# A sequence-mixing kernel's convolution: the last inverse stage by blocks of 32 channels, four product buffers, decays by products, and new order constants

## The chip, the cores and the metric

The kernel runs on one core of a Trainium2 chip. The metric is the device time of one execution in microseconds. The kernel before takes 688.63 us, the median of 3 runs (688.52 to 689.50). The engines are named as in the profile: PE (matrix products), DVE (vectors), ACT (scalar functions), POOL (general purpose) and SP, which issues most transfers.

## The reference

A block of a network on one sequence of 2048 positions and 512 channels: a long convolution per channel, whose taps come from 128 decaying oscillations a channel, and after it a mixer of four dense layers. Cut to what matters:

```python
x = A_u                                                # [1, 2048, 512]
n = layernorm(x)
dt = exp(log_dt); A = -exp(log_A_real) + 1j * A_imag   # [512, 128]
C = (C_real + 1j * C_imag) * dt[:, None]
K = 2 * einsum("dn,dnl->dl", C, exp((A * dt)[:, :, None] * arange(2048))).real
y = irfft(rfft(n, 4096) * rfft(K, 4096))[:2048]        # along the sequence
h = x + y + n * D_skip
out = h + B_ref(layernorm(h))      # two layers with shifts, then 512 -> 1792 -> 512
```

## The kernel before

The kernel has two phases. `conv_phase` computes `h`, which stays on the core as 16 tiles of 128 x 512; `mixer_phase` does the rest. The mixer starts with the last four tiles of `h` (`finish(3)`, `norm1(3)`, `turn1(3)`), so these are on its way first.

**Taps.** The 512 channels are done in 32 chunks of 16 (`table(g)`, `taps(s, g)`). The 2048 positions are split in two factors, so a chunk needs two small tables of sines and cosines times decays: ACT makes `pt` (sines and cosines of integer phases that POOL adds up), DVE or POOL multiply them by `amx` and `amy` into `cs` and `sn`, and PE multiplies the two tables into `kt`, 16 channels' taps. `SHARE` says which chunks' operations go to POOL or ACT instead of DVE: `amy`, `csy` and `sny` name chunks whose product is POOL's, `sq` chunks in which ACT squares part of `amx`. A list holds indices in a group of eight; the first list is for step 0 (`g < 8`), the second for all others. The decays are exponentials of the rates: `rates()` makes six for the low digits (`eb`) and, later, three for the high digits (`ec[:, :, 1]` to `ec[:, :, 3]`, with factors 512, 1024 and 1536). ACT's exponentials and its sines are in different table sets, which it has to load.

**Steps.** The channels are convolved in four steps of 128 (`WID`). In each the transform is done in two stages. `spectra_of_taps(s)` does stage A of the taps, by blocks of 64 channels, into `at[:, 1]`: either `stage_a_turn` (DVE transposes) or two `stage_a_taps` (more, smaller matmuls and copies by ACT); `SHARE["turn"]` lists the blocks of the first kind, by index 2s + r. `stage_a_x` does stage A of the input into `at[:, 0]`. For steps 2 and 3 (`FAR`) the input's whole spectrum is computed early (`spectrum_x`), sent to memory and fetched by `back`. Then for each of eight groups of frequencies `e`, `product(s, e)` does stage B on PE and multiplies both spectra into a buffer `u` (four partial products of a complex product), and `stage_b_inv(s, e)` transforms back into `at[:, 0]`. There are two buffers `u0` and `u1`, used in turn. `SHARE["sum..."]` lists the `e` whose four partial products are summed to two on DVE or POOL before; PE then needs two terms instead of four. `SHARE["mul..."]` lists the `e` whose product is POOL's.

After the eight groups `stage_a_inv` (steps 0 to 2) turns blocks of 32 channels on DVE into `u0` or `u1` and adds the last stage's result to `h`. The last step has `last_a_inv`: four transposes on DVE (`turn_inv`, r = 0 to 3, 32 channels each), then for each quarter `q` of the positions (in the order 3, 0, 1, 2) one product with the identity (`keep`) that puts `h` into a PSUM bank, four matmuls over 512 columns that add all 128 channels, and a copy to `h`. `q = 3` also goes through the statistics (`part`) that the mixer's first tiles need.

**x.** `norm_x()` takes the mean and variance of the 16 tiles on DVE, computes one root for all, and normalises: `SHARE["nrm"]` names two tiles for POOL, DVE takes the other four with j < `LND`, ACT ten.

**Order.** Nothing is issued as it stands in the source. `Plan.add` collects the instructions with a cost, what they read and write, and for some a constant `at`; `Plan.order` then places them engine by engine, and the engines run them in that order. Among an engine's instructions that can start within `LOOK` (0.05) of the earliest, it takes the one with the smallest due time, which is

```python
a["late"] = min([1e9 if a["at"] is None else a["at"]] + [N[j]["late"] - lag for j in succ[i]])
```

so the constants in `NOM` only rank instructions. `TS[s]`, the base of step s, is `t0` plus s times `per`; taps of step 0 are due at `kg0`, those of others at `TS[s - 1] + kg + ...`, the taps' stage A at `TS[s] - ak`, products at `TS[s] + b e`, inverses `ib` later, the early spectra at `xa + xs n`, the last stage's `keep` at `TS[4] + 15 + n` and its matmuls at `TS[4] + 20 + n`. Where PE would idle the plan puts matmuls with the identity as fillers, so that its clock stays up. PSUM banks are handed out by the plan; two pairs and two single ones are there.

## Time and profile before

| | us |
|---|---|
| median of the runs | 688.63 |
| the profiled execution | 688.2 |
| its span | 686.4 |
| PE busy | 650.4 |
| DVE busy | 547.6 |
| ACT busy | 408.0 |
| POOL busy | 404.9 |
| DVE busy from 0 to 305 | 274.8 |
| mean granted PE clock | 0.993 |

The convolution is roughly the first 305 us. All instructions of both phases carry the line L87, that of the helper through which they are issued, so groups are told apart by the tiles that they write and read: `pt`, `cs`, `sn`, `amx`, `amp` (which holds `amy`), `kt`, `at`, `u`, `bs`, `h`. `bank` is PSUM. A row of the timeline or of the chain starts with its start and duration; in a group's row stand count, busy time and mean in nanoseconds, then the idle time just before and what ended it. A row of the windows has the window and its length, the busy time of PE, PEld (weight loads), DVE, ACT and POOL, the granted clock, the share of the DMA engines and GB/s. A matmul of this type of number shows as two records.

### The profile page before, as it was taken

How to read it: one execution, taken by the hardware profiler on the slowest of the kernel's cores; microseconds unless marked ns; L12 is line 12 of the kernel's file. 1: busy time of each engine (PE TensorE's matmuls, PEld its weight loads, DVE VectorE, ACT ScalarE, POOL GpSimd, SP SyncE). 2: the span in 40 equal slices, each digit the busy share in tenths (PEclk: the TensorE clock that was granted, in tenths of full speed). 3: DMA queues.
4: the chain of work that ended last, by engine and by line, in shares of the span. 5: the costliest groups of instructions: out<-in, count | busy, mean ns of one | idle time of the engine just before them, and what ended most of it. 6: DMA issues, size and time to landing. Idle time of an engine off the chain costs nothing.

```text
span 686.4 us, 16787 instructions
## 1 busy us (share of the span) xinstructions
PE 650.4 (95%) x6806; PEld 507.3 (74%) x6806; DVE 547.6 (80%) x952; ACT 408.0 (59%) x706; POOL 404.9 (59%) x422
## 2 busy tenths in 40 slices
PE   5987989999999997999999999999999999999997
PEld 5885756663677584748888888888888888888885
DVE  5998899999897998989978798866879954455554
ACT  7889878967889876245634555544365443444330
POOL 1889589968999999002576209355635555554210
PEclk9998999999999999999999999999999999999999
DMA  8930554011301133020231311133311342211004
GB/s 224 268 128 2 168 174 110 3 48 32 64 3 49 34 95 110 1 63 1 62 93 48 106 32 47 46 97 103 96 44 46 101 129 62 62 46 47 21 11 122
DMA packets 49266, 51.49 MB, mean 75 GB/s; under 512 B 6437, under 2 KB 33061, under 8 KB 49189
## 3 DMA queue, kind: packets, MB, share of 16 engines
q1 hardware_dynamic: 47524, 47.80, 24.3%
q10 hardware_dynamic: 1152, 1.57, 0.9%
q0 software_dynamic: 512, 1.05, 0.6%
q8 instruction: 53, 0.87, 0.5%
q14 instruction: 25, 0.20, 0.1%
HBM read 35.72 MB, written 8.39 MB: 64 GB/s over the span
## 4 chain that ended last, share of the span: by engine, by line
PE 61%; ACT 13%; DVE 13%; POOL 4%; issue 4%; DMA 3%; SPq 2%; ACTq 0%; DVEq 0%; POOLq 0%
PE l L87 24%; PE acc L87 11%; ACT pt L87 8%; PE bank L87 6%; DVE u L87 4%; PE l3a L87 3%; PE l3g L87 3%; PE l3d L87 3%; PE l3f L87 3%; PE l3e L87 3%; PE l3c L87 3%; PE l3b L87 3%; DVE at L87 2%; SPq L347 2%; DVE cs L87 2%
## 5 line engine op out<-in xcount | busy, mean ns | idle before, releaser
L87 ACT ACTIVATE pt<-pt 128x1056 f32<-128x1056 int32 x64 | 69.8, 1091 | 14.5 <-POOL pt L87 6.3
L87 POOL TENSOR_TENSOR pt<-p,s 128x512 int32<-128x512 int32 x64 | 71.8, 1139 | 5.1 <-DVE sn L87 4.0
L87 PE MATMUL bank<-at,tbs 128*64 128x128 f32 (+1 forms) x768 | 63.1, 311 | 3.3 <-DVE u L87 1.8
L87 PEld LDWEIGHTS bank<-at,tbs 128*64 128x64 f32 x768 | 44.5, 134 | 20.6 <-ACT at L87 3.0
L87 PEld LDWEIGHTS bank<-ident 128*128 128x128 f32 x418 | 51.0, 200 | 8.3 <-issue 5.1
L87 PE MATMUL bank<-ident 128*128 128x128 f32 x418 | 55.1, 289 | 0.0
L87 PE MATMUL bank<-u,ms 64*128 64x128 f32 x768 | 50.6, 280 | 3.5 <-DVE at L87 1.3
L87 PEld LDWEIGHTS bank<-u,ms 64*128 64x128 f32 x768 | 45.4, 187 | 8.2 <-issue 1.8
L87 POOL TENSOR_TENSOR cs0w<-raw,cs0w 128x512 fp32r<-128x512 f32 x7 | 9.1, 1296 | 59.0 <-ACT cs0w L87 59.0
L87 DVE TENSOR_TENSOR cs<-pt,amx 128x512 f32<-128x512 f32 x64 | 40.9, 677 | 2.5 <-ACT pt L87 1.3
L87 DVE TENSOR_TENSOR h<-h,l 128x512 f32<-128x512 f32 x48 | 32.1, 684 | 11.0 <-PE l L87 11.0
L87 PEld LDWEIGHTS bank<-cs 128*32 128x32 f32 x1024 | 24.2, 111 | 22.5 <-POOL cs L87 6.1
L87 PE MATMUL bank<-cs 128*32 128x64 f32 x1024 | 32.7, 225 | 8.4 <-DVE cs L87 4.1
L87 POOL TENSOR_TENSOR sn1w<-raw,sn1w 128x512 fp32r<-128x512 f32 x7 | 9.5, 1359 | 52.1 <-ACT sn1w L87 41.7
L87 DVE TENSOR_TENSOR u<-u,l3f 128x512 f32<-128x512 f32 x14 | 9.5, 682 | 36.9 <-PE l3f L87 36.9
L87 ACT COPY at<-bank 128x512 f32<-128x512 f32 x40 | 24.9, 630 | 23.1 <-PE bank L87 23.0
L87 ACT ACTIVATE pt<-pt,halfpi 128x1056 f32<-128x1056 f32 x32 | 38.1, 1191 | 0.5
L87 POOL TENSOR_TENSOR sn<-pt,amp 128x512 f32<-128x512 f32 x30 | 36.8, 1227 | 1.4 <-ACT pt L87 1.1
L87 DVE STREAM_TRANSPOSE at<-bank 128x512 f32<-128x512 f32 (+1 forms) x40 | 35.6, 922 | 1.9 <-PE bank L87 1.9
L87 ACT ACTIVATE u<-u 128x512 f32<-128x512 f32 x56 | 35.4, 632 | 1.8
L87 PE MATMUL bank<-sn 128*32 128x64 f32 x1024 | 32.0, 223 | 2.5 <-DVE sn L87 2.5
L87 POOL TENSOR_TENSOR cs<-pt,amp 128x512 f32<-128x512 f32 x26 | 31.9, 1227 | 3.6 <-PE bank L87 1.1
(1159 smaller groups left out, 2082.9 us busy)
## 6 DMA issues: line engine op xcount, KB each, us to landing
raw<-in_B_w_dram SPq DMA_DIRECT2D x28, 256.0 KB, 2.8
xq<-xq SPq DMA_DIRECT2D x72, 64.0 KB, 2.0
h<-in_A_u_dram SPq DMA_DIRECT2D x32, 128.0 KB, 3.8
h<-in_A_u_dram SPq DMA_DIRECT2D x16, 256.0 KB, 4.1
rawa<-in_B_w_dram SPq DMA_DIRECT2D x14, 256.0 KB, 2.8
rawb<-in_B_w_dram SPq DMA_DIRECT2D x14, 256.0 KB, 2.9
ms<-in_mm_dram SPq DMA_DIRECT2D x4, 768.0 KB, 10.1
out_dram<-h SPq DMA_DIRECT2D x48, 64.0 KB, 1.7
```

The lines of the kernel that those rows point to most:

```text
L87: ins = f(*args, **kw)
L347: dma = lambda d, s: lambda: nc.sync.dma_start(d, s)
```

## The change

- **Last inverse stage.** `last_a_inv` issues all four `keep`, then the matmuls by blocks: for each r the four quarters q, over 128 columns (4 positions x 32 channels) instead of 512. A block needs only its own transpose; the bank is complete after r = 3.
- **Product buffers.** In the last step the `u` buffers are four: `thp` and `ini`, the phases' parameters, serve as the third and fourth once the tables are done.
- **High decays.** Only the factor 512 is an exponential, issued with the six others ahead of the first sine. The second is its square on ACT, the third the product of both on POOL. The later exponentials, and the change to their table set and back, go.
- **Parameters.** The first block's three copies out of PSUM go from ACT to DVE.
- **Statistics and normalisation of x.** `LNA = 4`: four tiles' sums and sums of squares are ACT's (two passes each). `LND = 4`, and no tile is normalised by POOL.
- **Shares.** `amy`, `csy`, `sny` and `sq` have a list for each step. In the last step the sums of e = 0, 1, 2, 5 go to POOL, those of 4, 6, 7 stay on DVE and 3 has none; the product of e = 4 goes to POOL. Step 0 loses the sums of e = 1 and 3. Block 2 (the first of step 1) is no longer turned by DVE.
- **Order.** `ak`, `ax`, `b`, `ib`, `y`, `ys`, `kg` and `kgs` get an addend for each step (`nom(n, s)`), the bases `TS` one for steps 1 to 3, and all constants have new values.

The diff, without the lines that only replace `NOM[...]` by `nom(...)`:

```diff
-SHARE = {'nrm': [[1], [5]], 'mul0': [[0], [7]], 'mul2': [[6], []], 'amy': [[0, 1, 3, 4, 5, 6, 7], [1, 2, 3, 6]], 'csy': [[1, 4, 5, 6, 7], [0, 1, 2, 3, 4, 5, 7]], 'sny': [[1, 2, 3, 5, 6, 7], [0, 1, 2, 3, 4, 5, 6, 7]], 'sq': [[0, 1, 5, 7], [0, 2, 3, 4, 6, 7]], 'turn': [[1, 2, 3, 5, 6, 7], [2, 3, 5, 6, 7]], 'hadd': [[0, 1, 2, 7], [0, 1, 2, 3, 5, 6, 7]], 'sum0': [[3], [1, 4, 6]], 'sum1': [[], [0]], 'sum2': [[], [4, 5, 6]], 'sum3': [[0, 1, 2, 3, 4, 5, 6, 7], []]}
+SHARE = {'nrm': [[], []], 'mul0': [[2], [7]], 'mul2': [[6], [4]], 'amy': [[0, 1, 2, 3, 4, 5, 6, 7], [0, 1, 2, 3, 6], [0, 2, 4, 6, 7], [3, 4, 6, 7]], 'csy': [[2, 3, 5, 6], [0, 1, 2, 3, 4, 5, 7], [0, 1, 2, 3, 4, 5, 7], [0, 1, 2, 3, 4, 5, 7]], 'sny': [[1, 2, 3, 5, 6, 7], [1, 2, 3, 4, 6, 7], [0, 1, 2, 3, 4, 6], [0, 1, 2, 3, 4, 5, 6, 7]], 'sq': [[0, 1, 2, 6], [0, 2, 3, 4, 5, 6, 7], [0, 1, 2, 4, 5, 6, 7], [0, 1, 3, 4, 5, 6, 7]], 'turn': [[1, 3, 5, 6, 7], [2, 3, 5, 6, 7]], 'hadd': [[0, 1, 2], [0, 1, 2, 3, 5, 6, 7]], 'sum0': [[], [4, 6]], 'sum1': [[], [0]], 'sum2': [[], [3, 4, 6]], 'sum3': [[4, 6, 7], [0, 1, 2, 5]]}
...
-LND = 5
-LNA = 0
+LND = 4
+LNA = 4
...
-NOM = {'t0': 20909.27, 'per': -2434.34, 'ln': 6742.44, 'kg0': -2181.49, 'kgs0': 3.82, 'kg': 15568.18, 'kgs': 8895.14, 'ak': 3925.33, 'ax': 241.48, 'b': 3.78, 'ib': -3456.91, 'y': 7609.31, 'ys': 1528.17, 'tr': 11007.37, 'exp': 6791.26, 'wt': 19369.85, 'pr1': 14609.18, 'pr2': 19765.45, 'st': 18836.53, 'xa': 5533.7, 'xs': -976.95}
+NOM = {'lna': -6411.31, 't0': 20522.35, 'per': -894.26, 'ln': -5822.64, 'kg0': -9318.19, 'kgs0': 3.78, 'kg': -2101.91, 'kgs': 25013.05, 'ak': 17752.48, 'ax': -220.66, 'b': 524.38, 'ib': -1943.3, 'y': 24805.75, 'ys': 7260.8, 'tr': 18844.68, 'exp': -1591.78, 'wt': 30586.62, 'pr1': 48035.89, 'pr2': 11141.85, 'st': 33977.18, 'xa': 4397.29, 'xs': -1767.73, 'kg.1': 38137.64, 'kg.2': 11471.49, 'kg.3': -9808.59, 'kgs.1': 22767.09, 'kgs.2': -6950.05, 'kgs.3': -1943.45, 'ak.0': -192.4, 'ak.1': 10223.63, 'ak.2': -15787.22, 'ak.3': 7962.67, 'ax.0': -11988.2, 'ax.1': 7758.29, 'ax.2': -8412.62, 'ax.3': 24117.63, 'b.0': 182.31, 'b.1': 415.63, 'b.2': -299.98, 'b.3': 33.97, 'ib.0': 152.15, 'ib.1': -1799.03, 'ib.2': 11285.45, 'ib.3': 39936.16, 'y.0': 12856.89, 'y.1': 6177.68, 'y.2': 23800.04, 'y.3': -15848.95, 'ys.0': -8274.72, 'ys.1': 11499.17, 'ys.2': -20246.8, 'ys.3': -37984.55, 't.1': 15629.02, 't.2': 3507.55, 't.3': 7837.49}
...
+    TS = [t + NOM.get(f"t.{i}", 0) for i, t in enumerate(TS)]
+    nom = lambda n, s: NOM[n] + NOM[f"{n}.{s}"]
...
-    decays += [(ec[:, :, k], 512.0 * k) for k in range(1, 4)]
+    decays += [(ec[:, :, 1], 512.0)]
...
-            for i, (d, m) in enumerate(decays[6:]):
-                add("ACT", 0.99 if i else 2.3, lambda d=d, m=m: act.activation(d, plan.view(p), AF.Exp, scale=-m), r=["lam"], w=["trig"], at=NOM["exp"])
-            add("ACT", 1.45, sine, w=["trig", "ex"], at=NOM["exp"], frees=p)
+            add("ACT", 0.99, lambda: act.activation(ec[:, :, 2], ec[:, :, 1], AF.Square), w=["ex"], at=NOM["exp"])
+            add("POOL", 1.2, lambda: gp.tensor_tensor(ec[:, :, 3], ec[:, :, 1], ec[:, :, 2], ALU.mult), w=["ex"], at=NOM["exp"])
...
+    uu += [t.rearrange("p g i d -> p (g i d)") for t in (thp, ini)]
+    PARAM = [("A", t) for t in R4] + [("I", t) for t in R4]
+
+    def turn_of(s, e):
+
+        k = e % (4 if s + 1 == NS else 2)
+        return uu[k], [("u", k)] + (PARAM if k > 1 else [])
...
-            def mm(q=q, view_=view_):
-                for c in R4:
-                    i = c % 2 * 16 + q * 4
-                    pe.matmul(view_()[quarter(c)], fis[:, c // 2, :],
-                              g[:, :, i : i + 4, :].rearrange("p d i t -> p i d t"), start=not KEEP, stop=True)
...
+        def mm(q, r):
+            b = plan.view(ps[q])[:, 0 : 4 * w_].rearrange("p (j d) -> p j d", j=4)
+            for c in R4:
+                i = c % 2 * 16 + q * 4
+                pe.matmul(b[quarter(c), :, r * 32 : r * 32 + 32], fis[:, c // 2, :],
+                          g[:, r * 16 : r * 16 + 16, i : i + 4, :].rearrange("p d i t -> p i d t"), start=False, stop=r == w_ // 32 - 1)
+
+        for r in range(w_ // 32):
+            for n, q in enumerate((3, 0, 1, 2)):
+                i = add("PE", 0.32, lambda q=q, r=r: mm(q, r), r=[("g", r), "fis"], w=[("hq", q)], at=TS[s + 1] + 20 + 4 * r + n)
...
-        a0 = 16 - LNA
-        for j in range(a0):
+        for j in range(LNA, 16):
             add("DVE", 0.6, lambda j=j: v.bn_stats(bx[:, j, :], h[:, j, :]),
...
-            for j in range(a0, 16):
+            for j in range(LNA):
                 add("ACT", 0.62, lambda j=j: act.activation(junk, h[:, j, :], AF.Copy, accum_out=sm[:, j : j + 1]),
-                    r=[("x", j // 2, c) for c in R4], w=[("u", 0), "sm"])
+                    r=[("x", j // 2, c) for c in R4], w=[("u", 0), "sm"], at=NOM["lna"])
```

96 lines of the change are left out of this document (48 added, 48 removed).

## The prediction

> **What bounds the kernel now.** I read the windows first, cut where the stages change, to see which engine is busiest in each; then the groups of instructions for prices, the chain of waits for 45 to 75 us, and the timeline of the last step.
>
> ```profile
> span 686.4 us, 16787 instructions
> ...
> 20.00:45.00 25.00, 22.49 (x307) 21.82 (x306) 23.96 (x61) 20.08 (x37) 20.39 (x23) 1.00 0.74 242
> 45.00:75.00 30.00, 25.11 (x495) 18.75 (x495) 26.77 (x36) 27.69 (x49) 28.39 (x25) 0.89 0.16 37
> 75.00:100.00 25.00, 23.40 (x568) 16.61 (x566) 22.87 (x52) 18.35 (x34) 15.94 (x17) 1.00 0.54 178
> 100.00:250.00 150.00, 140.41 (x2910) 94.47 (x2908) 138.24 (x204) 126.08 (x222) 134.64 (x133) 1.00 0.18 49
> 276.00:295.00 19.00, 18.53 (x257) 15.21 (x250) 18.42 (x31) 4.88 (x8) 0.00 (x0) 1.00 0.01 2
> 305.00:686.00 381.00, 376.95 (x1676) 311.28 (x1674) 272.83 (x473) 176.70 (x298) 176.84 (x191) 1.00 0.23 64
> ```
>
> The columns are PE, PEld, DVE, ACT, POOL. From 305 us to the end PE is 99% busy and the change leaves that code alone, so whatever moves the moment at which the mixer's first transposes start (304.79, below) moves the end by as much. Ahead of it, DVE is busiest (24.0 of 25 us, then 138.2 of 150), with POOL close behind (134.6 of 150). Much of PE's share there is filler, so its digits are no bound. The stretch 45 to 75 is ACT's and POOL's. In the last step DVE has 18.4 of 19 us and POOL nothing. So I count what each edit adds to DVE, POOL and ACT in each stretch.
>
> **Part 1, up to 75 us.** Four of 16 statistics go to ACT, two normalisations from POOL to ACT, high decays lose two exponentials and two table loads.
>
> ```profile
> L87 DVE BATCH_NORM_STATS2 bs<-h 128x6 f32<-128x512 f32 x16 | 10.4, 662 | 0.0
> L87 POOL TENSOR_SCALAR h<-h,mvh,bs 128x512 f32<-128x512 f32 x2 | 4.1, 2070 | 0.0
> L87 ACT COPY at<-bank 128x512 f32<-128x512 f32 x40 | 24.9, 630 | 23.1 <-PE bank L87 23.0
> L87 ACT ACT_TABLE_LOAD x4 | 5.1, 1283 | 0.8 <-PEq L1639 0.7
> L87 ACT ACTIVATE ec<-bank 128x512 f32<-128x512 f32 x3 | 3.2, 1144 | 0.0
> L87 ACT ACTIVATE h<-h,bs 128x512 f32<-128x512 f32 x10 | 7.4, 801 | 0.0
> ...
> 57.33 1.33 POOL h L87
> ...
> 59.41 2.06 POOL h L87
> ...
> 55.00:60.00 5.00, 1.81 (x49) 1.25 (x52) 4.02 (x8) 5.00 (x10) 4.89 (x4) 0.95 0.00 2
> 60.00:65.00 5.00, 4.31 (x64) 2.21 (x56) 3.65 (x8) 4.45 (x12) 5.00 (x5) 0.50 0.01 3
> 65.00:70.00 5.00, 5.00 (x108) 2.21 (x100) 4.58 (x6) 3.59 (x4) 5.00 (x5) 0.87 0.01 3
> ```
>
> DVE loses 4 x 0.66 = 2.65 us ahead of the root that all normalisations wait for, in a stretch where it is 96% busy. POOL loses 2 x 2.07, of which 1.33 + 2.06 = 3.39 us lie on the chain, just ahead of the transforms of x. ACT gains eight passes over 512 elements (price not shown with an accumulated output; between 0.63, the plain copy of that size, and 0.80, the normalisation's: 5.0 to 6.4 us, I take 5.7) and 2 x 0.80; it loses 2 x 1.28 and 2 x 1.14 and gains one squaring, at an exponential's 1.14. Net +3.6 us on an engine with 25 - 20.08 = 4.9 us idle from 20 to 45: that idle time covers it, and without the cover it is rival C. The multiplication on POOL (no longer than a normalisation's 2.07 there) is covered by the 4.1 us that POOL loses. The evacuation of the first parameter block moves three small copies to DVE, idle then; 0. Other shares of step 0 (one amplitude to POOL, one cosine back) cancel within 0.4 us. The two gains are the same wait seen from two sides (earlier root, shorter tail) and ACT's own queue of normalisations is what is late next, so I don't add them: **-2.65**, from -4.4 (-2.65 and the tail less ACT's two, 3.39 - 1.6) to +3.2 (rival C).
>
> **Part 2, steps 1 to 3's tables, 75 to 276 us.**
>
> ```profile
> L87 DVE TENSOR_TENSOR sn<-pt,amp 128x512 f32<-128x512 f32 x2 | 2.2, 1119 | 0.0
> L87 DVE TENSOR_TENSOR amp<-E,ec 128x512 f32<-128x512 f32 x13 | 10.1, 778 | 0.1
> L87 DVE STREAM_TRANSPOSE at<-bank 128x512 f32<-128x512 f32 x24 | 16.1, 703 | 0.0
> L87 DVE TENSOR_TENSOR amx<-E,amx 128x512 f32<-128x512 f32 x22 | 15.2, 691 | 5.9 <-ACT amx L87 5.8
> L87 DVE TENSOR_TENSOR amx<-E,amx 128x896 f32<-128x896 f32 x10 | 10.9, 1091 | 2.7 <-ACT amx L87 2.7
> L87 POOL TENSOR_TENSOR sn<-pt,amp 128x512 f32<-128x512 f32 x30 | 36.8, 1227 | 1.4 <-ACT pt L87 1.1 <-POOL pt L87 0.2
> L87 POOL TENSOR_TENSOR amp<-E,ec 128x512 f32<-128x512 f32 x19 | 21.4, 1131 | 6.0 <-DVE ec L87 5.6
> L87 POOL TENSOR_TENSOR u<-u 128x256 f32<-128x256 f32 x14 | 11.1, 818 | 0.8 <-DVE u L87 0.8
> 131.63 1.62 DVE L87 TENSOR_TENSOR u<-u 128x256 f32<-128x256 f32 x2
> 277.12 0.76 DVE L87 TENSOR_TENSOR u<-u 128x256 f32<-128x256 f32 x2
> ```
>
> DVE: four sine products come back (+4.48), two amplitudes go to POOL (-1.56), one block of taps is turned by PE and ACT instead of four transposes (-2.81), three more chunks leave part of the amplitudes to ACT's squares (3 x (1.09 - 0.69) = -1.20), the sum of e = 3 in step 0 goes (-1.62): -2.7 us. POOL: -4.9 for the sines, about +2.3 for the amplitudes, -1.6 for one pair of sums: -4.2. ACT +2.5 of copies (4 x 0.63) and three pairs of squares (put at DVE's shorter form, 0.69, together +2.1), against 24 us idle from 100 to 250. PE has two more four-term inverses, +2.1, under its fillers. The extra squares hardly add a wait: DVE idles 0.27 us ahead of either form (5.9/22, 2.7/10). DVE is 92% busy from 100 to 250, so -2.7 x 0.92 = -2.5, and 0.2 back for the waits: **-2.3**, from -4.2 (POOL sets the pace) to +1 (ACT's 4.6 us shows by about a quarter in place of the gain).
>
> **The order.** An instruction's due time is the smaller of its own constant and what its followers leave it. Worked out from the constants, the new taps of step 3 are due at 25677.06 - 17752.48 - 7962.67 = -38 and the end at about 16945 + 20; before, 9681 and 11192. Nearly every other new constant lies above what the followers give, so it decides nothing; as before, step 0's tables come first, then what leads to step 3's taps, then the rest. One thing moves: before, the spectra of x for steps 2 and 3 (due 4557 and 5534) went ahead of all tables of step 1; now (2630, 4397) their own constants lie behind and they interleave by length of path. That touches 75 to 100 us, where POOL idles 9 us and ACT 6.7 but DVE only 2.1. DVE's work is the cover: **0**, between -2.1 and +2.1.
>
> **Part 3, the last step, and part 4, its inverse by blocks.**
>
> ```profile
> 276.61 1.10 PE L87 MATMUL bank<-at,tbs 128*64 128x128 f32 x16
> 277.65 1.23 PE L87 MATMUL bank<-u,ms 64*128 64x128 f32 x16
> ...
> 292.96 1.16 PE L87 MATMUL bank<-u,ms 64*128 64x128 f32 x16
> ...
> 294.60 3.60 PE L87 MATMUL bank<-h,ident 128*128 128x512 f32 x8
> 294.80 4.63 DVE L87 STREAM_TRANSPOSE at<-at 128x1024 f32<-128x1024 f32 x4 [0.29 <-ACT at L87]
> ...
> 298.03 0.61 PE L87 MATMUL amx<-ident 128*128 128x128 f32 x4
> ...
> 299.48 4.72 PE L87 MATMUL bank<-at,fis 128*32 128x512 f32 x32 [0.84 <-DVE at L87]
> 300.87 0.89 DVE L87 BATCH_NORM_STATS2 bs<-bank 128x6 f32<-128x128 f32 x4 [1.45 <-PE bank L87]
> 301.19 0.14 PEld L87 LDWEIGHTS bank<-at,fis 128*32 128x32 f32 x4 [0.43 <-issue]
> 304.79 1.99 PE L87 MATMUL xt<-ident,xq 128*128 128x128 f32 x16 [0.59 <-DVE rn L87]
> 53.72 0.29 PE L87 MATMUL bank<-cs 128*32 128x64 f32 x8
> 53.83 0.29 PE L87 MATMUL bank<-sn 128*32 128x64 f32 x8
> ```
>
> DVE is relieved of five pairs of sums and one product, but PE is next: a product's matmuls and an inverse's take 1.04 us each (276.61 to 277.65), and from 276.61 to 294.0 seven of one and eight of the other make 15.6 of 17.4 us. The unsummed e = 3 adds 1.04. So four buffers can win at most 17.4 - 16.6 = 0.8 us; I take **-0.4**. Above: DVE's pair of sums took 1.62 us at 131.63 and 0.76 at 277.12, where POOL had nothing. POOL now works here too; three pairs at 0.86 more give +2.2. The Trainium skill (SBUF — State Buffer, on the shared port pair) says why: a DVE operation with two inputs in SBUF and a GpSimd one that reads SBUF lock each other out for the whole instruction. By that rule alone part 3 would be +2.2; the slower pair agrees, but DVE has the slack now.
>
> Part 4 looks like a gain, since the blocks need not wait for all four transposes. But what each block adds to, the four products with the identity, holds PE from 294.60 to 298.03 and is due earlier than every block. Then PE takes r = 0, 1, 2 for all four q before q = 3's last block, and q = 3 alone feeds the statistics at 300.87. A quarter of the 4.72 us for one r is 1.18: 298.03 + 3.25 x 1.18 = 301.87, where the old q = 3 was done at 299.48 + 1.18 = 300.66. That is **+1.2**. Ends: at the taps' pace (eight records of 64 columns in 0.11 us, 0.88 an r) 300.89, +0.2; with the 0.14 us load bare ahead of every four (0.14 + 0.43/4, twice for each q, 2.0 an r) 304.5, +3.9. A gain (-0.9, the last block 0.3 after the last transpose at 299.43) needs the blocks ahead of the products with the identity.
>
> **Sum:** -2.65 - 2.3 + 0 - 0.4 + 1.2 = -4.15 from the profiled execution's 688.2 (span 686.4 and 1.8 around it): 684.05. The median of the runs is 0.43 above that execution, so **684.5**.
>
> **The rivals.**
> A, *the clock falls at the handover* (0.17). PE would finish its blocks at 298.03 + 4.7 = 302.7 and wait until 304.79 + 1.2 = 306.0. From 55 to 60 us PE was busy 1.8 of 5, and the clock went to 0.50 and 0.87, some 6.8 us at half speed. Ahead of a PE-bound stretch 3.4 to 6.8 us at half cost 1.7 to 3.4: 684.5 + 2.5 = 687.0. Against it: 3.3 us of idle time is near the least that can do it. The Trainium skill (TensorE: Matmul & The Clock Gate, Part 1) puts the window at about 3.4 us, free-running; by that rule the idle time may or may not fill one, and the dip here agrees with it.
> B, *all reliefs count* (0.15): -4.4 - 4.2 - 0.8 + 0.2, 9.2 less, 679.4. For it: DVE and POOL are both lightened. Against: ACT is not.
> C, *the statistics on ACT come last* (0.20), the slower side. They are due behind all of step 0's tables (-6411 against -9318) on an in-order engine. ACT needs 5.7 + 1.6 more; the 4.8 us that the decays free lie ahead of 21 us, when x is still landing. If they can't be used, 7.3 us meet 4.9 idle and ACT is over 90% busy from 45 on, so the normalisation ends 2.4 later, and the small operations that turn sums into moments, put at 0.8, with it: +3.2. DVE's relief is then half waited away (-1.2), and 688.6 + 3.2 - 1.2 - 0.4 + 1.2 = 691.4. It decides from 5 us of ACT work that finds no gap before 45.
> The forecast itself holds 0.48.
>
> **How the numbers follow.** No change can be told within 0.2%, 1.4 us: 687.25 to 690.0. The forecast's own range, 681.5 to 687.5, gives 0.46 faster and 0.02 same; A 0.10 and 0.07; B 0.15; C 0.04 same and 0.16 slower. Together 0.71, 0.13, 0.16. The range runs from just under B to C, 679 to 691.5.
>
> **What would show it.** Part 1: the last normalisation before 60 us and no clock dip there; if the root comes after 40, C. Part 2: DVE some 2.5 us less busy between 75 and 276, with POOL's idle time up. Part 3: products and inverses back to back on PE at 1.04. Part 4: q = 3's statistics about 7.3 us after the first of the four transposes, where 300.87 - 294.80 = 6.1 before; 5.2 would make it wrong. A: a granted clock below 1.00 just after the handover. Two or more of parts 1 to 3 gaining nothing would make the whole wrong.

## The result, and the profile after

The kernel with the change takes 690.11 us, the median of 22 runs (687.15 to 691.99), the kernel before 688.36 in the 22 runs beside them (687.26 to 689.62). The ratio is 1.0022, with an interval of 1.0012 to 1.0033: slower by 1.5 us by the ratio (0.8 to 2.3), 1.75 by the medians. The forecast was 684.5, so the time lies inside the range of 679 to 691.5 and on the wrong side of the time before.

The profiled execution of the changed kernel took 689.71 us. Its windows follow, with the columns of before (PE, PEld, DVE, ACT, POOL, granted clock, DMA share, GB/s). In this kernel the helper's line is L86.

```profile
span 687.9 us, 17248 instructions
...
20.00:45.00 25.00, 20.93 (x282) 20.40 (x282) 23.47 (x49) 22.66 (x48) 21.13 (x22) 0.94 0.80 254
45.00:75.00 30.00, 22.51 (x413) 15.28 (x412) 25.90 (x34) 25.80 (x46) 24.30 (x24) 0.77 0.10 27
75.00:100.00 25.00, 22.82 (x591) 15.51 (x588) 23.18 (x52) 19.94 (x37) 14.70 (x16) 1.00 0.50 163
100.00:250.00 150.00, 141.29 (x3184) 96.74 (x3180) 137.22 (x201) 130.04 (x233) 132.18 (x130) 0.98 0.20 52
276.00:295.00 19.00, 18.50 (x269) 15.40 (x270) 14.34 (x21) 5.89 (x10) 11.85 (x13) 1.00 0.01 2
305.00:686.00 381.00, 377.22 (x1676) 311.54 (x1676) 274.41 (x477) 176.84 (x298) 176.20 (x191) 1.00 0.24 64
```

The mixer behind 305 us is as it was. Ahead of it the engines' shares moved as planned (ACT +4.0 and POOL -2.5 us between 100 and 250, DVE -4.1 and POOL +11.9 in the last step), but the clock from 45 to 75 is worse, 0.77 where it was 0.89, and 0.98 from 100 to 250 where it was 1.00.

To see where time was won and lost I took from the timeline of DVE the start of the n-th scalar-tensor-tensor operation that writes `sn`, one for each of the 32 tables in order of time, and the start of the mixer's first transposes (`xt`), in us of each kernel's profiled execution:

| | 4th | 8th | 9th | 16th | 18th | 20th | 32nd | `xt` |
|---|---|---|---|---|---|---|---|---|
| before | 50.24 | 74.73 | 96.01 | 152.39 | 166.87 | 184.72 | 262.43 | 304.79 |
| after | 53.80 | 79.96 | 97.09 | 152.21 | 167.00 | 186.90 | 263.54 | 306.20 |
| after minus before | +3.6 | +5.2 | +1.1 | -0.2 | +0.1 | +2.2 | +1.1 | +1.4 |

The +5.2 at the eighth table is not all time lost, because the new order does other work ahead of it: by then DVE has begun 42 operations on the parameters (those that write `scratch`, `thp`, `ini` or `ec`), before only 28, and it has been busy for 68.2 us instead of 63.4. At the ninth table, behind that work in both kernels, 1.1 us are left. So three things are to be explained: 1.1 us lost by the ninth table though x is normalised earlier; 2 us lost around 180, so that the 32nd table comes as late as the ninth; and the end, where `xt` comes 1.4 late.

**Up to 75 us.** The timeline of the changed kernel, rows of the normalisation, of PE and of DVE:

```profile
35.81 1.08 DVE L86 SCALAR_TENSOR_TENSOR bs<-mvh,bs 128x16 f32<-128x16 f32 x1
...
41.33 3.52 DVE L86 TENSOR_SCALAR h<-h,mvh,bs 128x512 f32<-128x512 f32 x4
...
54.71 0.80 ACT L86 ACTIVATE h<-h,bs 128x512 f32<-128x512 f32 x1
...
59.00 0.90 ACT L86 COPY kt<-bank 128x256 f32<-128x256 f32 x3
...
59.40 0.90 PE L86 MATMUL bank<-ident,at 128*128 128x128 f32 x3 [1.61 <-ACT kt L86]
60.23 1.96 PE L86 MATMUL bank<-h,fas 32*32 32x512 f32 x16
...
64.48 1.24 DVE L86 STREAM_TRANSPOSE at<-bank 128x1024 f32<-128x1024 f32 x1
```

The root is done at 36.9 (before, 40.1) and the last tile is normalised at 55.5 (before, 61.5): 6 us earlier. But PE begins x's transform at 60.23 instead of 61.53, since taps wait ahead of it for ACT's copies; and DVE's first transpose of x starts at 64.48, at the moment of before (64.44), with no wait written beside it: it stands behind tables in DVE's order. The first row shows another loss: the last small operation of the root takes 1.08 us, where it took 0.19 before.

**From 75 to 276 us.** Some of the groups of DVE up to 305 us, first of the changed kernel, then, as they were before, the two of an unchanged count that grew most:

```profile
L86 DVE TENSOR_TENSOR u<-xs,bank 128x1024 f32<-128x1024 f32 x23 | 27.9, 1220 | 3.3 <-ACT xs L86 2.2 <-PE bank L86 1.1
...
L86 DVE STREAM_TRANSPOSE at<-bank 128x512 f32<-128x512 f32 x20 | 12.9, 697 | 0.7 <-PE bank L86 0.7
...
L86 DVE BATCH_NORM_STATS2 bs<-h 128x6 f32<-128x512 f32 x12 | 7.8, 680 | 0.2 <-DMA dsk<-in_A_D_skip_dram 0.2
L86 DVE TENSOR_TENSOR sn<-pt,amp 128x512 f32<-128x512 f32 x6 | 5.2, 866 | 0.0
L86 DVE TENSOR_TENSOR scratch<-scratch 128x128 f32<-128x128 f32 x10 | 4.4, 463 | 0.1
L86 DVE TENSOR_TENSOR kt<-kt,dsk 128x16 f32<-128x16 f32 x8 | 3.6, 448 | 0.5 <-ACT kt L86 0.5
```

```profile
L87 DVE TENSOR_TENSOR scratch<-scratch 128x128 f32<-128x128 f32 x10 | 2.7, 285 | 0.4 <-ACT scratch L87 0.3
L87 DVE TENSOR_TENSOR kt<-kt,dsk 128x16 f32<-128x16 f32 x8 | 1.9, 235 | 1.1 <-ACT kt L87 1.1
```

The counts are those of the change: 20 transposes for 24, 12 statistics for 16, six sines for two. But DVE's busy time up to 305 us falls by 5.5 (274.8 to 269.3), where the counted reliefs make 10.4: 2.65 of statistics, 2.7 of tables, and in the last step five pairs of sums at 0.76 and a product at 1.2. Small operations with unchanged counts took 3.4 us more in the two groups above alone, and 4.5 us more over all groups of an unchanged count (7.3 more in some, 2.8 less in others). That is about what they lose beside POOL: added up over DVE's operations that start while one of POOL's runs, the time above the shortest of the same form is 25.5 us before and 30.2 after. Where DVE waits has moved too: ahead of its products it idles 3.3 us (before, 0.8), mostly for ACT's copies of the spectrum.

**Around 180 us.** PE in the timeline of the changed kernel, then two windows that are cut where the granted clock changes:

```profile
174.14 1.00 PE L86 MATMUL bank<-fas,kt 32*64 32x32 f32 x53
177.05 0.42 PE L86 MATMUL bank<-fas,kt 32*64 32x32 f32 x11 [1.90 <-issue]
...
178.19 5.37 PE L86 MATMUL bank<-at,tbs 128*64 128x256 f32 x32
```

```profile
175.13:178.55 3.42, 1.44 (x21) 1.11 (x20) 3.42 (x6) 1.97 (x6) 3.42 (x3) 1.00 0.02 5
178.55:181.96 3.41, 3.41 (x20) 1.91 (x18) 2.20 (x3) 2.51 (x4) 2.87 (x4) 0.50 0.01 2
```

In the middle of a group of equal matmuls, behind 128 records of tables and 53 of taps in 3.1 us, PE idles 1.90 us with nothing named that it waits for ("issue"). In a stretch of 3.42 us it is busy for 1.44; in the next 3.41 us the clock is at 0.50, and step 2's first two products take 5.37 us. Before, they took 3.69.

**The end.** The last inverse in the timeline of the changed kernel:

```profile
294.85 3.60 PE L86 MATMUL bank<-h,ident 128*128 128x512 f32 x8
295.06 4.81 DVE L86 STREAM_TRANSPOSE at<-at 128x1024 f32<-128x1024 f32 x4 [1.67 <-ACT at L86]
...
298.38 4.71 PE L86 MATMUL bank<-at,fis 128*32 128x128 f32 x128
...
302.30 0.89 DVE L86 BATCH_NORM_STATS2 bs<-bank 128x6 f32<-128x128 f32 x4 [2.43 <-PE bank L86]
...
306.20 1.99 PE L86 MATMUL xt<-ident,xq 128*128 128x128 f32 x16 [3.11 <-DVE rn L86]
```

The statistics of q = 3 start 7.24 us after the first of the four transposes (before, 6.07). PE is through with its blocks at 303.1 and then idles 3.11 us for the mixer's first tile.

**How the clock falls.** In every profile of this study the stretches at half clock up to 320 us are 3.41 us long or a multiple of it, and lie on a grid of 3.41 us, whose place against the kernel's start differs from run to run. I cut the stretch from 28 to 318 us of 20 profiles by each run's own grid and compared PE's busy share in a window with the clock in the next. At full clock, of 44 windows with a share under 0.485 the clock fell after 43, of 17 between 0.485 and 0.6 after 4, of 259 between 0.6 and 0.85 after 12 (all of these hold 28 or more small matmuls of a transform of taps, `bank<-fas,kt`), of 1242 above that after none. At half clock it stayed there after all 54 windows with a share under 0.85, and rose after 58 of 60 above. So it is not a gap of some length that counts but half a window without work, and whether a gap fills half a window depends on where the grid lies. The two windows of the changed kernel that share the wait at the handover:

```profile
301.43:304.84 3.41, 1.66 (x48) 1.32 (x40) 2.30 (x16) 2.07 (x4) 0.00 (x0) 1.00 0.00 0
304.84:308.25 3.41, 2.02 (x17) 1.73 (x17) 3.23 (x10) 1.49 (x3) 0.00 (x0) 1.00 0.00 0
```

The grid cuts the wait in the middle. Each window has 0.49 and 0.59 of PE's work, and the clock stays. The Trainium skill (TensorE: Matmul & The Clock Gate, Part 1) gives a free-running window of 3413 ns, and the grid agrees with it: the shortest stretches at half clock are recorded as 3413 ns. Its rule that an idle window is needed does not agree: up to 0.48 of PE's work in one was little enough.

### The profile page after: what moved, and what is told of

It is laid out like the page before. It is cut to its first block, busy times and chain, and to the rows that moved or that the text cites. A ratio compares the mean times of both kernels' runs of the same rounds, so it can differ in the third digit from the quotient of the medians.

```text
span 687.9 us, 17248 instructions
## 1 busy us (share of the span) xinstructions
PE 642.3 (93%) x7036; PEld 502.7 (73%) x7036; DVE 543.7 (79%) x932; ACT 414.7 (60%) x731; POOL 406.5 (59%) x427
## 4 chain that ended last, share of the span: by engine, by line
PE 67%; DVE 13%; ACT 11%; issue 3%; DMA 2%; POOL 2%; SPq 0%; ACTq 0%; DVEq 0%; POOLq 0%
PE l L86 24%; PE bank L86 12%; PE acc L86 11%; ACT pt L86 6%; DVE cs L86 3%; PE l3g L86 3%; PE l3d L86 3%; PE l3f L86 3%; PE l3e L86 3%; PE l3c L86 3%; PE l3b L86 3%; PE l3a L86 3%; DVE sn L86 2%; DVE u L86 2%; DMA h<-in_A_u_dram 2%
## 5 line engine op out<-in xcount | busy, mean ns | idle before, releaser
L86 POOL TENSOR_TENSOR pt<-p,s 128x512 int32<-128x512 int32 x64 | 73.3, 1161 | 6.2 <-DVE sn L86 5.8
L86 ACT ACTIVATE pt<-pt 128x1056 f32<-128x1056 int32 x64 | 69.8, 1090 | 11.8 <-DVE cs L86 5.4
L86 PE MATMUL bank<-at,tbs 128*64 128x128 f32 (+1 forms) x768 | 64.5, 316 | 3.0 <-ACT at L86 0.6
L86 PEld LDWEIGHTS bank<-at,tbs 128*64 128x64 f32 x768 | 45.5, 136 | 20.0 <-issue 2.6
L86 PE MATMUL bank<-u,ms 64*128 64x128 f32 x736 | 47.2, 278 | 3.3 <-ACT at L86 1.3
L86 PEld LDWEIGHTS bank<-u,ms 64*128 64x128 f32 x736 | 42.9, 188 | 7.8 <-DVE u L86 2.0
L86 PE MATMUL bank<-cs 128*32 128x64 f32 x1024 | 33.0, 228 | 11.8 <-ACT kt L86 4.0
L86 POOL TENSOR_TENSOR cs0w<-raw,cs0w 128x512 fp32r<-128x512 f32 x7 | 9.1, 1294 | 58.9 <-ACT cs0w L86 58.9
L86 PEld LDWEIGHTS bank<-cs 128*32 128x32 f32 x1024 | 24.6, 113 | 25.6 <-issue 6.7
L86 DVE TENSOR_TENSOR cs<-pt,amx 128x512 f32<-128x512 f32 x64 | 41.1, 677 | 0.9 <-ACT amx L86 0.3
L86 POOL TENSOR_TENSOR sn1w<-raw,sn1w 128x512 fp32r<-128x512 f32 x7 | 9.5, 1359 | 53.3 <-ACT sn1w L86 53.3
L86 DVE TENSOR_TENSOR h<-h,l 128x512 f32<-128x512 f32 x48 | 32.0, 684 | 10.6 <-PE l L86 10.6
L86 ACT COPY at<-bank 128x512 f32<-128x512 f32 x44 | 27.2, 629 | 20.9 <-PE bank L86 20.9
L86 PE MATMUL bank<-ident 128*128 128x128 f32 x284 | 38.8, 297 | 0.0
L86 DVE TENSOR_TENSOR u<-u,l3f 128x512 f32<-128x512 f32 x14 | 9.6, 682 | 37.0 <-PE l3f L86 37.0
L86 PEld LDWEIGHTS bank<-ident 128*128 128x128 f32 x284 | 36.2, 208 | 3.4 <-issue 1.4
L86 ACT ACTIVATE pt<-pt,halfpi 128x1056 f32<-128x1056 f32 x32 | 37.8, 1183 | 0.4
L86 ACT ACTIVATE u<-u 128x512 f32<-128x512 f32 x56 | 35.4, 633 | 1.8
L86 POOL TENSOR_TENSOR cs<-pt,amp 128x512 f32<-128x512 f32 x25 | 31.0, 1239 | 8.0 <-DVE amp L86 3.3
L86 POOL TENSOR_TENSOR sn<-pt,amp 128x512 f32<-128x512 f32 x26 | 31.7, 1218 | 6.6 <-issue 4.3
L86 DVE STREAM_TRANSPOSE at<-bank 128x512 f32<-128x512 f32 (+1 forms) x36 | 32.4, 942 | 2.8 <-PE bank L86 2.7
L86 DVE TENSOR_TENSOR amx<-E,amx 128x512 f32<-128x512 f32 (+1 forms) x32 | 24.8, 774 | 10.5 <-ACT amx L86 10.4
```

What stands on the lines that cost most here:

```text
L86: ins = f(*args, **kw)
```

## The experiments

All ratios are to the runs of the kernel before beside them, with their 95% intervals. Times in the diffs, such as 180.1, name instructions by the order's own clock and are no device times.

**The change split in two.** The whole change with the last inverse as before, and, from the other side, the kernel before with the inverse by blocks alone.

```diff
 # e1_whole, against the changed kernel: as before, one instruction for each q
+    for c in R4: pe.matmul(view_()[quarter(c)], fis[:, c // 2, :], g[:, :, i : i + 4, :]...)
 # e17_blocks, against the kernel before: the change's last_a_inv
+    for r in range(w_ // 32):
+        for n, q in enumerate((3, 0, 1, 2)):
+            add("PE", 0.32, ..., at=TS[s + 1] + 20 + 4 * r + n)
```

> The changed kernel with its last inverse stage as before, four whole products of 512 columns. If the blocks cost what the trace of the changed kernel shows (11.14 us from the first of the four transposes to the mixer's first one, against 9.99 before), this gives 1.15 us back: 690.1 - 1.15 = 689.0 us, still not faster than 688.4. If the whole loss of 1.75 us lies in the blocks, it gives 688.4 or less. If the blocks cost nothing, 690.1.

> The kernel before with the change's last inverse stage alone, by blocks of 32 channels; everything ahead of it keeps its order. Part 4 by itself, on a kernel whose runs spread by 2.4 us and not by 4.8: statistics of q = 3 7.2 us after the first of the four transposes (6.07 in the kernel before), time 688.3 + 1.15 = 689.5, from 689.2 to 689.8. If the blocks cost nothing here, the difference seen in the changed kernel came from its clock: 688.0 to 688.6.

Without the blocks the change takes 687.68 us, ratio 0.9998 (0.9984 to 1.0011): no difference that can be told, the interval is 1.1 us faster to 0.8 us slower. The blocks alone take 690.22, ratio 1.0029 (1.0017 to 1.0041), +2.0 us, more than the 1.15 worked out for them. So the whole loss is the last inverse's, and no gain of all the rest of the change shows in the medians. The profile of the blocks alone shows both what they cost always and what they cost in some executions; timeline and windows:

```profile
294.11 4.82 DVE L87 STREAM_TRANSPOSE at<-at 128x1024 f32<-128x1024 f32 x4 [0.29 <-ACT at L87]
...
297.44 4.70 PE L87 MATMUL bank<-at,fis 128*32 128x128 f32 x128
301.38 0.89 DVE L87 BATCH_NORM_STATS2 bs<-bank 128x6 f32<-128x128 f32 x4 [2.44 <-PE bank L87]
...
305.28 3.65 PE L87 MATMUL xt<-ident,xq 128*128 128x128 f32 x16 [3.14 <-DVE rn L87]
```

```profile
300.80:304.22 3.42, 1.34 (x40) 1.01 (x31) 2.57 (x17) 2.06 (x4) 0.00 (x0) 1.00 0.01 2
304.22:307.63 3.41, 2.35 (x11) 2.38 (x12) 3.17 (x10) 0.82 (x1) 0.00 (x0) 0.50 0.00 0
307.63:311.04 3.41, 3.41 (x13) 2.93 (x12) 2.74 (x5) 3.34 (x5) 0.00 (x0) 0.50 0.00 0
```

The statistics come 7.27 us after the first transpose, as in the changed kernel. But here the grid lies otherwise: a window has 1.34 of 3.42 us of PE's work (0.39), the clock falls inside the wait of 3.14 us and, as the next window is only 0.69 full, stays down for two. The transposes take 3.65 us instead of the 1.99 that they took in the changed kernel after a wait of 3.11.

**The order of the blocks.** All blocks of q = 3 due first, in the changed kernel and on the kernel before.

```diff
-                ... at=TS[s + 1] + 20 + 4 * r + n)
+                ... at=TS[s + 1] + 20 + (4 * r if n else 0) + n)
```

> The changed kernel; in the last inverse stage the four blocks of q = 3 go ahead of all blocks of the other three. If Part 4's account is right, that q = 3's last block stands behind twelve others: its statistics 5.3 to 5.8 us after the first of the four transposes (7.24 in the changed kernel, 6.07 before), the mixer's first transposes 1.5 us earlier than in the changed kernel, time 688.0 to 688.9. If the others' blocks, now last, are what the mixer waits for: 689.5 to 690.5.

> The kernel before with the last inverse stage by blocks and q = 3's blocks ahead of the others. Statistics 5.3 to 5.8 us after the first of the four transposes, time 687.6 to 688.0, 0.3 to 0.7 faster than before. If the other blocks, now behind q = 3's last transpose, come late for what follows: 688.3 to 689.

In the changed kernel this takes 687.46 us, ratio 0.9994 (0.9981 to 1.0007), 1.9 less than the change; on the kernel before 687.36, ratio 0.9980 (0.9967 to 0.9992), which beats both kernels. The timeline on the kernel before:

```profile
294.22 4.70 DVE L87 STREAM_TRANSPOSE at<-at 128x1024 f32<-128x1024 f32 x4 [0.29 <-ACT at L87]
...
297.54 1.04 PE L87 MATMUL bank<-at,fis 128*32 128x128 f32 x24
298.97 3.90 PE L87 MATMUL bank<-at,fis 128*32 128x128 f32 x104 [0.39 <-DVE at L87]
299.51 0.89 DVE L87 BATCH_NORM_STATS2 bs<-bank 128x6 f32<-128x128 f32 x4 [0.60 <-PE bank L87]
...
303.44 2.25 PE L87 MATMUL xt<-ident,xq 128*128 128x128 f32 x16 [0.57 <-DVE rn L87]
```

The first 24 records are three blocks of q = 3; the fourth follows the last transpose. The statistics come 5.29 us after the first transpose, and PE, which has the other quarters' blocks meanwhile, waits 0.57 us where it waited 3.14: the fall of the clock has no place any more.

**Single due times and shares.** Three attempts to undo one part of the change in the source: a due time for step 0's tap copies, the order constants of before, and x's statistics and normalisation of before.

```diff
 # e2_kt
-  add("ACT", 0.27, lambda: act.copy(k, ...), w=[key], frees=p)
+  add("ACT", 0.27, lambda: act.copy(k, ...), w=[key], frees=p, at=nominal + 1.5 if s == 0 else None)
 # e3_nom: NOM of before, all addends 0
 # e4_x
-SHARE = {'nrm': [[], []], ...   LND = 4   LNA = 4
+SHARE = {'nrm': [[1], [5]], ... LND = 5   LNA = 0
```

> The changed kernel; ACT's eight copies of step 0's tap banks (kt) get a due time just behind the tap products', so that they stand ahead of the normalisations of x, where the changed kernel has them behind (first copy at 55.4 us, 35.7 before). Theory 1, that these late copies hold the four one-bank slots, starve PE and delay step 0's tables by 5 us: first copy near 40 us, the eighth table near 75 us and not 80, the four last transposes near 291 us, time 685 to 687.5. Theory 2, that the four statistics on ACT or the shares are what is late: copies earlier, time within 1 us of 690.1.

> The changed kernel with the order constants of before, every addend of a step at 0, the statistics on ACT due with the normalisations. Theory 1 (the new constants cost the upstream gain of 5 us): 685 to 687. The prediction's own term for the constants (0, from -2.1 to +2.1): 688 to 692. Rival, that the constants fit the new shares and are worth something: above 692.

> The changed kernel with the treatment of x as before: sixteen statistics on DVE, two normalisations on POOL, five on DVE; the new order constants stay. If four statistics on ACT (3.2 us there ahead of the first sines) are what delays step 0's tables: first sine near 20.8 us and not 22.3, time 686 to 688. If the constants are the cause, the tap copies still come behind the normalisations and the time stays at 689.5 to 692, since DVE has its 2.65 us of statistics back.

They took 697.52 (1.0162, 1.0134 to 1.0190), 708.06 (1.0289, 1.0265 to 1.0314) and 701.57 us (1.0199, 1.0185 to 1.0214). None of these times is the price of the part that its name gives: each edit re-orders all engines to the end of the convolution. They show something else, and plainly: the shares and the constants belong together, and the new shares under the old constants cost 18 us more than under the new. All later edits therefore move instructions in the finished order, or change what one of them does, and leave the rest.

**Up to 75 us, with the order kept.** Step 0's tap copies moved up on ACT as soon as their product is there; the normalisations of x taken in another sequence around 45 us; and, on the kernel with q = 3 first, the four statistics given back to DVE in ACT's places.

```diff
 # e6_kt: each copy with "early" is put ahead of ACT's first instruction that starts after its product
+  out.insert(k, i)
 # e10_norms: DVE's four and ACT's normalisations of x change places with their neighbours
+  for t in (41.7, 40.2, 38.9, 38.0): put(at("DVE", t), at("DVE", 44.0))
+  for t in (44.6, 43.8, 43.1): put(at("ACT", t), at("ACT", 47.4))
+  put(at("ACT", 48.3), at("DVE", 44.0))
 # e15_stats, against e11_q3
-  add("ACT", 0.62, lambda j=j: act.activation(junk, h[:, j, :], AF.Copy, accum_out=...), ...)
+  add("ACT", 0.62, lambda j=j: v.bn_stats(bx[:, j, :], h[:, j, :]), ...)
```

> The changed kernel; step 0's tap copies are moved up in ACT's order to just behind the tap products that they empty, and every other instruction keeps its place on every engine (a due time, as in the second run, reshuffled everything behind). Theory 1: first copy at 35 us, clock 1.00 up to 57, step 0's last table before 78, and median 686 to 688. Theory 3: the same up to 75 us, but the later dips stay, and median 689.5 to 690.5.

> The changed kernel; around 45 us the four normalisations of x on DVE (3.52 us in a row) go behind the third table's four operations, and three of five on ACT, with the copy that the fourth table's amplitudes wait for (2.92 us on DVE), change places with that table's three phase operations; everything else keeps its place. Theory 4, that the treatment of x put into step 0's tables is what takes Part 1's gain: the fourth table 1.5 to 2.5 us earlier (53.8 before), the eighth 1 to 2 earlier than 80.0, and the time 688 to 689. If something behind 75 us sets the pace anyway: the tables earlier and the time within 0.7 of 690.1.

> As the run with q = 3's blocks first, and the statistics of the four tiles that the change gave to ACT are taken by DVE again, each at the place that ACT's pass had; ACT's eight passes fall away, and the order is otherwise that of the changed kernel. If Part 1 was right that DVE's 2.65 us count: 689 to 690.5, step 0's tables later. If ACT's passes (5.4 us and 1.5 of accumulator reads) are what delays these tables, so that the edit cost as much as it saved: tables earlier, 685.5 to 687.5.

With the copies moved up the kernel takes 689.28, ratio 1.0013 (1.0000 to 1.0026) against the change's 1.0022: some 0.6 us less, and the intervals overlap. In that profile (timeline) x's transform starts earlier, and the transpose does not:

```profile
58.04 1.96 PE L86 MATMUL bank<-h,fas 32*32 32x512 f32 x16
...
64.02 1.24 DVE L86 STREAM_TRANSPOSE at<-bank 128x1024 f32<-128x1024 f32 x1
```

The matmuls are 2.2 us ahead of the changed kernel's, the transpose 0.5: DVE's own queue holds it. The other sequence of the normalisations was slower (691.91, 1.0050, 1.0035 to 1.0064), and the fourth and eighth tables, which it should have brought forward, came 0.9 and 1.1 us later (54.69 and 81.06). With the statistics back on DVE the kernel takes 688.49, ratio 1.0000 (0.9987 to 1.0012) against 0.9994 with them on ACT: about 0.4 us, and the intervals overlap, so no gain of theirs in time is established, though the ninth table comes 1.0 us later without it (98.16 for 97.16).

**Fillers.** The changed kernel has fewer matmuls with the identity, and its clock is lower. So twelve were put back at three places, and, from the other side, sixteen taken from the kernel before at its places between 150 and 175 us; one kernel has the fillers, the earlier copies and the whole inverse.

```diff
 # e5_fill
+  more = {148.2: 5, 167.7: 4, 169.7: 3}
 # e8_nofill, against the kernel before
+  none = self.nodes[i]["eng"] == "PE" and round(self.nodes[i]["start"], 1) in (150.3, 159.7, 173.3)
```

> The changed kernel with twelve filler products more (of ident, one bank each): five ahead of step 1's first inverse, four ahead of a tap transform of step 2 and three ahead of step 2's first product; nothing else moves. There the changed kernel has two filler products between 143 and 175 us of its plan, the kernel before seventeen, and its granted clock falls to 0.69 (155 to 160 us) and 0.80 to 0.85 (175 to 185); its 22 runs spread with the mean clock (0.976: 692, 0.987: 687.4). Theory 3, the missing gain is lost in these two stretches because PE has too little work ahead of them: clock 1.00 there, mean above 0.985, median 686 to 687.5. Theory 1 (late tap copies and step 0): 689 to 691, since the first dip, 50 to 70 us, stays.

> The kernel before without sixteen of its filler products: six ahead of step 1's first inverse, five ahead of its third, five ahead of step 2's first product. Theory 3: granted clock below 0.9 in 155 to 160 or in 175 to 185, runs spread over more than 3 us, median 690 to 692.5. If fillers there decide nothing: 688.0 to 688.8, or a little faster, since 16 x 0.23 us of PE's time fall away.

> The changed kernel with the twelve filler products, the moved tap copies and the last inverse stage as before, in whole products. If the three are worth what they were each expected to be (3, 0 to 2, 1.15 to 1.6): 684 to 686, below both kernels. If the clock falls at another place instead: 687 to 689.

Neither side supports the theory that the fillers are what is missing. With twelve more: 695.48, ratio 1.0103 (1.0088 to 1.0119); with sixteen less: 688.39, ratio 1.0000 (0.9991 to 1.0009). The combination, 696.28 (1.0112, 1.0099 to 1.0126), keeps the loss. In the profile of the kernel with twelve more the changed kernel's fall of the clock at 154.65 is gone, that at 178.55 is still there (178.47), and a new one comes far from the places of the fillers:

```profile
260.39:263.80 3.41, 0.35 (x8) 0.00 (x0) 1.21 (x2) 2.71 (x5) 2.72 (x3) 1.00 0.25 74
263.80:267.22 3.42, 3.35 (x80) 1.92 (x80) 3.42 (x7) 1.52 (x4) 3.26 (x4) 0.50 0.34 93
```

PE has 0.35 of 3.41 us to do, and the clock halves for the next window (and one more). In the changed kernel's profile the clock stays at 1.00 there. But it also falls near there, at 261.56 and 261.95, in two kernels without these fillers (the earlier copies and, below, the transfers held back), so they are not shown to be what thins this window, nor where all of the 5 us go.

**Around 180 us.** Two ways to take away PE's wait of 1.90 us, if it waits for its own instructions: four transfers of x held back to a later moment, so that nothing is loaded just then; and, on the kernel with q = 3 first, one of the two tap products put behind step 2's first product, so that fewer small matmuls come in a row.

```diff
 # e9_reload: SP's four re-loads are put behind an ACT instruction that writes one column of their target
+  for t in (169.4, 166.6, 163.8, 161.0): put(at("SP", t), hold)
 # e13_burst, against e11_q3
+  put(at("PE", 166.3), at("PE", 169.7))
+  out.insert(out.index(at("ACT", 173.1)) + 1, copy)
```

> The changed kernel; the four transfers that load a quarter of x again (issued at 168.8 us, when the DMA engines show a share of 1.02 from 170 to 175) are held back by one small ACT copy to about 189 us; nothing else moves. The changed kernel's PE waits 1.90 us for its own instructions at 175 to 177 (0.2 us in all of the kernel before), and its next two products then take 5.37 us at a granted clock of 0.80 to 0.85, where two took 3.69 before. If these transfers slow the loading of PE's instructions: that wait falls under 0.4 us, the products take 3.7, time 686.5 to 688.5. If PE's burst of small matmuls alone does it (128 in two tap products and 64 in a transform of taps, in a row): the wait stays at 1.2 to 1.9 us and the time at 689 to 690.5.

> As the run with q = 3's blocks first (687.46 us), and one of the two tap products that stand in a row ahead of step 2's transform of taps goes behind step 2's first product, with its ACT copy. If the 128 small matmuls in a row make PE wait for its instructions (1.54 us there, 1.90 in the changed kernel) and make the clock fall now and then just behind: wait under 0.6 us, the first product of step 2 about 2 us earlier than 176.90, spread of the runs smaller than 4.3 us, time 685.5 to 686.7. If the wait only moves behind the product, or the tap product is late for its table: 687 to 689.

With the transfers held back the wait falls from 1.90 to 0.91 us, and the time does not: 689.71, ratio 1.0029 (1.0016 to 1.0041). With the burst split the wait is gone. PE in the timeline of the split kernel:

```profile
172.87 1.13 PE L86 MATMUL bank<-fas,kt 32*64 32x32 f32 x64 [0.86 <-DVE at L86]
...
175.86 1.96 PE L86 MATMUL bank<-at,tbs 128*64 128x256 f32 x16 [1.22 <-ACT at L86]
```

The product starts at 175.86 instead of 176.90 in the kernel with q = 3 first alone. But another wait, for ACT, has taken the place, and by the 32nd table 0.24 us of this 1.04 is left (261.05 against 261.29). The median is 687.65 against 687.46 us, the ratio 0.9984 (0.9967 to 1.0000) against 0.9994: not told apart. The runs, which were to spread less than 4.3 us, spread over 6.2.

The kernel with q = 3 first alone shows what these 2 us are. It issues the same as the changed kernel up to the last inverse, but in its profile the grid lies otherwise (timeline, then a window):

```profile
175.76 0.42 PE L86 MATMUL bank<-fas,kt 32*64 32x32 f32 x11 [1.54 <-issue]
...
176.90 3.69 PE L86 MATMUL bank<-at,tbs 128*64 128x256 f32 x32
```

```profile
175.00:180.00 5.00, 4.16 (x43) 2.82 (x44) 4.27 (x6) 4.30 (x9) 5.00 (x6) 1.00 0.01 3
```

PE has the same kind of wait here, 1.54 us, but the clock stays, and the 20th table comes at 184.65, as before (184.72). So the 2 us belong to one execution in which the clock falls, and not to the order as such. The whole stretch of steps 1 to 3's tables shows the same in three kernels that issue the same up to the last inverse:

| | falls of the clock in the stretch | 9th to 32nd table | first of the four transposes |
|---|---|---|---|
| before | none | 166.42 | 294.80 |
| changed kernel | at 154.65 and 178.55 | 166.45 | 295.06 |
| last inverse as before | at 154.58 | 164.92 | 293.40 |
| q = 3 first | none | 164.13 | 292.83 |

Without a fall the change is 2.3 us faster there, with one 1.5, with two not at all. These are single profiles; in the medians little of it is left.

**DVE's small additions.** On the kernel with q = 3 first, the stretched additions to `kt` of steps 1 to 3 went to POOL.

```diff
-  add("DVE", 0.1, lambda: v.tensor_tensor(k0, k0, d, ALU.add), r=["dsk"], ...
+  add("DVE", 0.1, lambda: (gp if s else v).tensor_tensor(k0, k0, d, ALU.add), r=["dsk"], ...
```

> As the run with q = 3's blocks first, and the small additions to the taps (kt<-kt,dsk) of steps 1 to 3 go from DVE to POOL. On DVE they take 172 ns alone and up to 1047 where POOL is at work on SBUF; the eight cost 3.6 us, 1.9 in the kernel before. If DVE time lost to POOL in this way (4.6 us more than before, over all forms, up to 276 us) is what took Part 2's gain: 685.5 to 686.8. If DVE's loss there is hidden by other waits: 687 to 688.

That costs 1.4 us: 689.34, ratio 1.0015 (1.0004 to 1.0027).

**Several edits together.** One kernel has the earlier copies, the transfers held back, the other sequence of normalisations and q = 3 first; another the earlier copies, the transfers, q = 3 first, the split burst and the additions on POOL.

> The changed kernel with the moved tap copies, the moved treatment of x, the transfers held back and q = 3's blocks first. If each gives its part (0.8, 1 to 2, 2 to 3, 1.5): 683 to 685, below both kernels. If one dip of the clock is only traded for another: 687 to 689.

> As the run with q = 3's blocks first, with the tap product behind the first product, the additions on POOL, the tap copies of step 0 moved up and the transfers held back. If the waits that these remove lie on one chain: 683.5 to 685.5, below both kernels. If each is covered by the next: 686.5 to 688.

They take 688.75 (1.0006, 0.9995 to 1.0016) and 688.62 (1.0006, 0.9991 to 1.0022): no better than q = 3 first by itself. But each holds an edit that by itself cost time, the other sequence of the normalisations or the additions on POOL; the rest without these two was not run. The best version found is the kernel before with the blocks, q = 3 first, at a ratio of 0.9980.

## Why the prediction was wrong

**Part 4, the blocks (+1.2): right, in mechanism and in the trace's number.** The products with the identity do go first, q = 3 does come last, and its statistics start 7.24 us after the first transpose, where 7.3 was worked out; against before that is +1.17. The medians show more, 1.65 us (ratios 1.0022 and 0.9998 with and without the blocks) to 2.0. The surplus of 0.5 to 0.8 us fits rival A, but was not measured by itself.

**Rival A, the clock at the handover: right as a mechanism, wrong as an alternative.** It is no other case beside the forecast but something that these blocks make likely. Nine kernels of this study issue the blocks in the change's order, and in all nine profiles PE waits 3.11 to 3.16 us there; in six the clock falls and the mixer's first transposes take 2.60 to 3.65 us, in three, the change's among them, it does not and they take 1.99. The step that failed is "3.3 us of idle time is near the least that can do it": by the windows some 1.8 us in one of them is enough. Its price of 2.5 us is the upper end. In the profile of the blocks alone, from the start of the mixer's first transposes to that of the products `l<-xt33h,cs0w`, it takes 6.37 us (305.28 to 311.65), in the changed kernel's 3.99 (306.20 to 310.19): 2.4 more. In the other five profiles with a fall it is 1.1 to 1.3.

**Part 1 (-2.65): failed.** The working priced an earlier root and an earlier end of the normalisation, and both came: 3.2 and 6 us earlier. Yet the ninth table, the first behind step 0, comes 1.1 us later. The step that failed is that the normalisation is what x's transform waits for. It was so by 0.69 us in the trace of before, and only for PE; right behind it stood PE's and DVE's own orders, and the transpose of x started at 64.48 for 64.44. That there would be "no clock dip there" was wrong as well: with PE's share of 22.5 in 30 us instead of 25.1 the clock is at 0.77. The statistics alone, with the order kept, are worth 0.4 us or nothing. ACT's eight passes were priced at 5.0 to 6.4 us; with the reads of their sums they take 6.9. Rival C fell too: the root was done at 36.9, not behind 40. What makes up the 1.1 us was not found: of three edits up to 75 us one made the ninth table earlier, by 0.7 (the copies, 96.42).

**Part 2 (-2.3): right in size where the clock stays, and lost where it falls.** The counts were right. Between the ninth and the 32nd table the new shares, with the new order, take 164.13 us without a fall of the clock, where the kernel before takes 166.42: the 2.3 that were forecast. In the changed kernel's own profile they take 166.45, with two falls. The step that failed is "Much of PE's share there is filler, so its digits are no bound", so that the sum has no term for PE's clock: a window of small matmuls at 151.24 us (0.83 of it busy) and a thin one at 175.13 (0.42) are followed by half clock, and the tables behind them come later. Why the new order has such windows was not shown, and putting fillers back did not help. The way to the 2.3 was not as worked out either, so that its size came out is partly luck. POOL's idle time went up by 6.1 us between 75 and 276, but DVE's busy time there fell by 0.34 (184.58 to 184.24) instead of 2.5; up to 305 us it fell by 5.5 of 10.4, as operations that stayed took longer beside POOL. That stretching costs time at the end is not shown: the one experiment on it was slower.

**The order (0): the claim failed, and the sign is open.** That nearly every other new constant decides nothing was argued from the rule for due times; with the constants of before the same shares take 708.06 us. The new constants are what makes the new shares level with the old ones, so a value of 0 between -2.1 and +2.1 priced a thing that has no price by itself.

**Part 3 (-0.4): its mechanism was right.** PE in the timeline of the changed kernel, just behind step 2's last inverse:

```profile
278.71 1.10 PE L86 MATMUL bank<-at,tbs 128*64 128x128 f32 x16
279.75 1.16 PE L86 MATMUL bank<-thp,ms 64*128 64x128 f32 x16
...
293.19 1.18 PE L86 MATMUL bank<-ini,ms 64*128 64x128 f32 x16
```

Products and inverses follow each other at 1.04 to 1.09. From the first product behind step 2's last inverse to the products with the identity it is 16.14 us (278.71 to 294.85), before 17.99 (276.61 to 294.60). One of these 1.85 us is a product that PE had done earlier, so some 0.8 are the relief, the bound that was given. The interval from the 32nd table to the first of the four transposes says the same: 31.5 us for 32.4. It was not a gain at the end, because step 2's last inverse itself came 2.1 us later (277.50, before 275.41). The price put on slower sums beside POOL (+2.2) was not put to the test: DVE's pairs lie almost wholly where POOL idles, and two of the three took 0.76.

**The sum.** Parts 1 to 3 were to bring the first of the four transposes 5.35 us forward. It comes 2.0 us earlier in the profile without a fall between the ninth and the 32nd table (+1.1 of Part 1, -2.3 of Part 2, -0.8 of Part 3), 1.4 earlier with one fall and 0.3 later with two, and in the medians the change without its blocks brings 0.1 (0.9998). Then come the +1.2 of the blocks and, in some executions, the fall at the handover, which make the time longer than before. The sentence that two or more parts gaining nothing would make the prediction wrong comes near this case, and rival B, in which all reliefs count, was the farthest off.

**What stays open.** The change's runs spread over 4.8 us, those of before over 2.4, and go with the mean granted clock: over 22 runs the correlation is -0.90, and 0.01 of clock is worth 3.9 us. The grid would explain such a spread: in the thin stretches of PE (around 150, 177, 260 and 304 us in these kernels) the clock falls in some profiles and not in others, also between kernels that issue the same there. In the profile of before the clock falls only once ahead of the mixer, at 59.5 for 6.8 us; with the change it falls there for 13.7 us, at 55.7, and before that for 3.4 at 42.0. Whether more work for PE in that first stretch would bring the time below that of before was not tried: the fillers went to later places.
